# Infini-attention beside sliding-window attention: ordering the last phase by query tile

## Chip, core and metric

The kernel runs on one core of one Trainium2 chip. The metric is device time in microseconds (us) from the launch of the program to its end. A profile of one execution shows the engines: PE (TensorE), DVE (VectorE), ACT (ScalarE), POOL (GpSimd) and SP (SyncE, which here issues the DMAs).

## What is computed

Two attention layers over 2,048 tokens of width 640, 32 heads of 20, each with its own input; the results stand side by side in an output of 2048 x 1280. Cut to what matters:

```python
# A: four segments of 512; within a segment causal softmax attention, and a read of a running memory
logits = einsum('bhqd,bhkd->bhqk', qs, ks) * scale + mask
a_dot = einsum('bhqk,bhkd->bhqd', softmax(logits), vs)
a_mem = (phi(qs) @ M) / (phi(qs) @ z + 1e-06)        # phi(t) = t + 1 if t > 0 else exp(t)
o = g * a_mem + (1 - g) * a_dot                      # g = sigmoid(beta), one per head
M += phi(ks)^T vs;  z += sum(phi(ks))
out_A = o @ wo
# B: sliding window of 256 keys
scores = where(0 <= i - j < 256, q k^T * scale, -1e9)
out_B = (softmax(scores) @ v) @ wo
```

## The kernel before

The tokens are four chunks (NC = 4) of 512, each of four tiles (CT = 4) of 128. The work is eight phases, B and A in turn for chunks 0 to 3; the last phase is A, chunk 3. The 32 heads are eight groups (G) of four. A Unit (L31) is one group in one phase.

**Packs.** A Phase (L47) lists its packs. A pack is a list of entries (unit, key tile, offset, first query tile, number of query tiles) that together fill 512 columns. `scores` (from L451; matmuls at L459) computes keys x queries for four heads, each head on its own 32 rows of PE, into two PSUM buffers "Sc" of two heads each (three exist). ACT turns each into exponentials (L465) in a tile "pt" (six exist); POOL zeroes what the causal mask forbids on the diagonal block (L479). Phase A has 20 full packs. In phase A a unit's entries cover key tiles 0 to 3 with 4, 3, 2 and 1 query tiles.

**From exponentials to output.** When all packs of a unit are issued, and two packs later (LAG), `weigh` (L495) multiplies them with v: output columns are the tokens, output rows the 20 head dimensions and the softmax sum, four heads on 32 rows each (matmuls L514) into a PSUM buffer "D" (two exist, shared with all other dense work). DVE evicts it as "oc" (L527), a DMA transpose on SP's queue turns it to tokens on partitions, "ocT" (L529), and three packs later in the last phase `normalise` (L540) takes the reciprocal of the sum (L544), multiplies (L549) into "otA" and, in phase A, adds the memory's part "omem" (L561; for groups 0 to 4 together, then group by group). After group 7 the phase's four tiles are ready for output: `prefetch` turns them by DMA transposes "oT" (`turn`, L571), at most three at a time, and `out_step` computes half a tile (five matmuls L580, DVE eviction L583), with a store after the second half (L587).

**Order.** `body` (L656) issues everything by hand, pack by pack: what was put down for this slot (`after`), scores, one weighing if one is ready, prefetch, then dense work picked by cost. The dense work of the last phase is eight reads of the memory (`read`, L415: matmuls L435, DVE L442 to L445 into omem) and the output halves that OUT_TILES allows: 8 tiles here, a tile two slots after its turn at the earliest. Each engine and the SP queue work in the order of issue.

**The end.** Before the last pack's scores, groups 0 to 4 of the chunk are turned on PE (`last_turn` for column blocks 0 to 2: L616, copies L623). After them `tail` (L736) weighs groups 6 and 7, turns them on PE (`turn_here`, matmuls L536), normalises them, turns column blocks 3 and 4 (L616, L620, L621) and multiplies all four tiles with wo (`last_mm`, L628), the first three blocks in between, and stores them (L641, L643, L646).

Of the kernel before, what the change touches and what calls it, by code (L numbers as in the profile page):

```python
# [27 lines left out]
OUT_TILES = (0, 0, 3, 2, 6, 3, 7, 8)  # L28
# [3 lines left out]
class Unit:  # L32


    def __init__(self, br, c, g):
        self.br, self.c, self.g = br, c, g
        self.left = 0
        self.work = []
# [11 lines left out]
class Phase:  # L50

    def __init__(self, br, c):
# [4 lines left out]
        if br == "A":  # L57
# [20 lines left out]
        for p in self.packs:  # L78
            for e in p.entries:
                e[0].left += 1  # L80


class Kern:
# [367 lines left out]
    def scores(self, pk, last=False):  # L451
# [15 lines left out]
        for (u, kt, off, q0, nq) in pk.entries:  # L467
            loc = kt - u.c * CT
            if last:
                b = off + loc - q0  # L470
                blk = pt[:, 0:2, b * P:(b + 1) * P]
                nc.gpsimd.affine_select(out=blk, in_=blk, pattern=[[0, 2], [1, P]],
                                        compare_op=ALU.is_ge, fill=0.0, base=0,
                                        channel_multiplier=-1)
                self.open_masks.append(pt[:, 2:4, b * P:(b + 1) * P])
            elif 0 <= loc - q0 < nq:
                b = off + loc - q0
                blk = pt[:, :, b * P:(b + 1) * P]
                nc.gpsimd.affine_select(out=blk, in_=blk, pattern=[[0, 4], [1, P]],  # L479
                                        compare_op=ALU.is_ge, fill=0.0, base=0,  # L480
                                        channel_multiplier=-1)
# [6 lines left out]
        for e in pk.entries:  # L488
            u = e[0]
# [4 lines left out]

    def weigh(self, u):  # L495
        nc = self.nc
        O = self.dtile([P, CH], F32)
# [22 lines left out]
        if self.closing:  # L520
            if u.g == G - 1:
                nc.scalar.copy(out=oc[:, 0:256], in_=O[:, 0:256])
                nc.vector.tensor_copy(out=oc[:, 256:512], in_=O[:, 256:512])
            else:
                nc.vector.tensor_copy(out=oc[:], in_=O[:])
            return oc
        nc.vector.tensor_copy(out=oc[:], in_=O[:])  # L527
        tp = self.wk.tile([P, CT, P], BF16, name="ocT", bufs=4)
        nc.sync.dma_start_transpose(out=tp[:], in_=oc[:])  # L529
        late = 3 if u.br == "A" and u.c == NC - 1 else 4  # L530
        self.at(self.slot + late, lambda: self.normalise(u, tp))

    def turn_here(self, u, oc):
        tp = self.dtile([P, CT, P], BF16)
        for b in range(CT):
            self.nc.tensor.transpose(out=tp[:, b, :], in_=oc[:, b * P:(b + 1) * P],  # L536
                                     identity=self.ident[:])
        self.normalise(u, tp)

    def normalise(self, u, tp):  # L540
        nc = self.nc
        pv = tp[:].rearrange("p b (j c) -> p b j c", j=4)
        rr = self.wk.tile([P, CT, 4], F32, name="rr", bufs=2)
        nc.vector.reciprocal(out=rr[:], in_=pv[:, :, :, DH])  # L544
        if u.g == 0:
# [3 lines left out]
        nc.vector.tensor_tensor(out=o[:, :, cols].rearrange("p b (j e) -> p b j e", j=4),  # L549
                                in0=pv[:, :, :, 0:DH],  # L550
                                in1=rr[:].unsqueeze(3).to_broadcast([P, CT, 4, DH]),
                                op=ALU.mult)
        if u.br == "A" and u.c > 0:
# [6 lines left out]
            if cols.stop > cols.start:  # L560
                nc.vector.tensor_tensor(out=o[:, :, cols], in0=o[:, :, cols],  # L561
                                        in1=self.omem[:, :, cols], op=ALU.add)
        if u.g == G - 1:
            self.tiles += [(u.br, u.c, tt) for tt in range(CT)]
# [40 lines left out]
    def last_turn(self, br, c, m0, m1):  # L605

        nc = self.nc
        o = self.o_tok[br, c]
        if m0 == 0:
            self.oTs = self.wk.tile([P, KT, CT, P], BF16, name="pkt", bufs=1)  # L610
        n = 2 if m0 == 0 else 4
        for a in range(0, CT, n):
            ps = self.dtile([P, m1 - m0, n, P], BF16)
            for i in range(n):
                for m in range(m0, m1):
                    nc.tensor.transpose(out=ps[:, m - m0, i, :],  # L616
                                        in_=o[:, a + i, m * P:(m + 1) * P],
                                        identity=self.ident[:])
            if m0:
                nc.vector.tensor_copy(out=self.oTs[:, m0:m1, 0:2, :], in_=ps[:, :, 0:2, :])  # L620
                nc.scalar.copy(out=self.oTs[:, m0:m1, 2:4, :], in_=ps[:, :, 2:4, :])  # L621
            else:
                nc.vector.tensor_copy(out=self.oTs[:, m0:m1, a:a + 2, :], in_=ps[:])  # L623

    def last_mm(self, br, tt, m0, m1):
        for hf in range(2):
            for m in range(m0, m1):
                self.nc.tensor.matmul(self.last[tt][hf], lhsT=self.oTs[:, m, tt, :],  # L628
                                      rhs=self.w[br + "o"][:, m, hf * 320:(hf + 1) * 320],
                                      start=(m == 0), stop=(m == KT - 1))  # L630

    def last_sc(self, tt):
        ps = self.ps.tile([P, 2, CH], F32, name="Sc", bufs=3)
        self.last[tt] = [ps[:, 0, 0:320], ps[:, 1, 0:320]]
        return ps

    def last_store(self, br, c, tt, ps, eng):
        nc = self.nc
        ot = self.wk.tile([P, 2, 320], BF16, name="ot" if tt < 3 else "oT", bufs=3 if tt < 3 else 4)
        if eng is nc.scalar:  # L640
            nc.scalar.copy(out=ot[:], in_=ps[:, :, 0:320])  # L641
        else:
            nc.vector.tensor_copy(out=ot[:], in_=ps[:, :, 0:320])  # L643
        r0 = c * CH + tt * P
        c0 = 0 if br == "A" else D
        nc.sync.dma_start(out=self.out2d[r0:r0 + P, c0:c0 + D],  # L646
                          in_=ot[:].rearrange("p a b -> p (a b)"))
# [8 lines left out]
    def body(self):  # L656
# [3 lines left out]
        self.closing, self.open_masks = False, []  # L660
        for n, ph in enumerate(phases):
# [12 lines left out]
            for i, pk in enumerate(ph.packs):  # L674
# [7 lines left out]
                if last:  # L682
                    self.last_turn("A", NC - 1, 0, 3)
# [33 lines left out]
        self.tail("A", NC - 1)  # L717
# [18 lines left out]
    def tail(self, br, c):  # L736

        nc = self.nc
        self.closing, self.last, ps = True, {}, {}
        (_, u), (_, w) = self.ready  # L740
        assert not self.tiles
        ou = self.weigh(u)
        for blk in self.open_masks:
            nc.vector.tensor_tensor(out=blk, in0=blk,
                                    in1=self.cmask[:].unsqueeze(1).to_broadcast([P, 2, P]),
                                    op=ALU.mult)
        while self.turned or self.half:
# [5 lines left out]
        ps[0] = self.last_sc(0)  # L753
        self.last_mm(br, 0, 0, 3)
        self.turn_here(u, ou)
        ps[1] = self.last_sc(1)
        self.last_mm(br, 1, 0, 3)
        ow = self.weigh(w)
        ps[2] = self.last_sc(2)
        self.last_mm(br, 2, 0, 3)  # L760
        self.turn_here(w, ow)
        self.last_turn(br, c, 3, KT)
        for tt in range(3):
            self.last_mm(br, tt, 3, KT)
            self.last_store(br, c, tt, ps[tt], (nc.scalar, nc.vector)[tt % 2])
        ps[3] = self.last_sc(3)
        self.last_mm(br, 3, 0, KT)
        self.last_store(br, c, 3, ps[3], nc.vector)
# [50 lines left out]
```

## Time and profile before

| what | value |
|---|---|
| median of 3 runs | 392.62 us (392.05 to 395.66) |
| the profiled execution | 390.19 us |
| its span on the core | 388.1 us |
| granted PE clock | 0.99 of full speed |
| busy over the span: PE, DVE, ACT, POOL | 88%, 71%, 87%, 65% |
| first exponential of the last phase | 338.67 us |
| last two exponentials start | 373.28 and 374.20 us |
| last store issued | 385.33 us |

All times inside the profile count from the start of the span; about 2 us lie around it. A row of the order of time gives start, duration, engine, line, operation, output and inputs, and in brackets how long the engine had idled and what ended that.

### The profile page before, as it was taken

The page shows a single profiled execution, that of the slowest core. Times are in us where ns is not written, and L with a number is a line of the kernel's source. Part 1 is how long each engine was busy: PE and PEld are TensorE (multiplying, and loading weights), DVE is VectorE, ACT ScalarE, POOL GpSimd, SP SyncE. Part 2 cuts the span into 40 slices and gives each one's busy share as a digit, 9 for nine tenths or more (in the row PEclk, how much of TensorE's full clock was granted, in tenths as well). Part 3 has the DMA queues.
Part 4 walks back from the last instruction along what each step waited for, and adds up shares of the span by engine and source line. Part 5 has one row for each costly group of instructions (what it writes and reads, how often), then busy time and mean ns, then how long its engine had stood idle before and what let it go on. Part 6 is the DMA issues. An engine that isn't in the chain of part 4 may idle for free.

```text
span 388.1 us, 10554 instructions
## 1 busy us (share of the span) xinstructions
PE 340.4 (88%) x4060; PEld 161.3 (42%) x4060; DVE 276.7 (71%) x581; ACT 338.1 (87%) x384; POOL 251.8 (65%) x392
## 2 busy tenths in 40 slices
PE   7999988977998798988997989898999989988884
PEld 3433434322443344444543335444454435544442
DVE  2467667634788868788778886789877887777583
ACT  2867789985999889888999999988999999999972
POOL 9657564542777587635578888844458988955550
PEclk9999999998999989999999999999999999999999
DMA  8993328647434597728575697758474377736312
GB/s 256 314 285 77 47 83 151 113 105 187 134 80 134 143 173 141 135 71 137 117 135 135 127 190 126 149 104 110 116 146 120 92 169 129 113 78 113 96 30 70
DMA packets 110738, 50.77 MB, mean 131 GB/s; under 512 B 81760, under 2 KB 110688, under 8 KB 110688
## 3 DMA queue, kind: packets, MB, share of 16 engines
q1 hardware_dynamic: 110688, 50.10, 61.1%
q8 instruction: 32, 0.52, 0.6%
q14 instruction: 18, 0.15, 0.1%
HBM read 16.39 MB, written 14.42 MB: 79 GB/s over the span
## 4 chain that ended last, share of the span: by engine, by line
PE 42%; ACT 24%; DVE 16%; issue 6%; POOL 6%; DMA 3%; SPq 0%; POOLq 0%; DVEq 0%; ACTq 0%
ACT pt L465 22%; PE D L267 13%; PE Sc L459 7%; PE D L326 6%; PE D L580 5%; PE D L514 5%; PE D L253 4%; POOL pt L479 3%; DVE qk L270 3%; POOL pt L485 3%; DVE oc L527 3%; ACT pe L310 2%; PE Sc L628 2%; DVE omem L445 1%; DMA ocT<-oc 1%
## 5 line engine op out<-in xcount | busy, mean ns | idle before, releaser
L465 ACT ACTIVATE pt<-Sc 128x1024 bf16<-128x1024 f32 (+1 forms) x344 | 320.7, 1077 | 32.3 <-PE Sc L459 28.2
L479 POOL TENSOR_SCALAR_AFFINE_SELECT pt<-pt 128x512 bf16<-128x512 bf16 x254 | 167.6, 671 | 117.2 <-ACT pt L465 116.9
L485 POOL TENSOR_SCALAR_AFFINE_SELECT pt<-pt 128x512 bf16<-128x512 bf16 x112 | 78.6, 717 | 5.1 <-ACT pt L465 4.8
L270 DVE CAST qk<-D 128x512 bf16<-128x512 f32 x70 | 47.9, 687 | 29.4 <-PE D L267 26.8
L527 DVE CAST oc<-D 128x512 bf16<-128x512 f32 x62 | 42.7, 688 | 19.9 <-PE D L514 19.8
L459 PE MATMUL Sc<-qpB,kpB 20*128 20x256 bf16 (+2 forms) x704 | 43.3, 277 | 7.8 <-ACT pt L465 4.7
L459 PE MATMUL Sc<-qpA,kpA 20*128 20x384 bf16 (+3 forms) x512 | 41.0, 302 | 5.8 <-ACT pt L465 5.0
L580 PEld LDWEIGHTS <-oT 128*128 128x128 bf16 x280 | 25.4, 98 | 17.9 <-issue 6.6
L583 DVE CAST ot<-D 128x320 bf16<-128x320 f32 x56 | 27.0, 485 | 7.2 <-PE D L580 6.4
L459 PEld LDWEIGHTS <-kpB 20*128 20x128 bf16 x704 | 13.6, 92 | 42.5 <-issue 38.5
L267 PE MATMUL D<-xTA,Aq 128*128 128x512 bf16 x100 | 24.9, 379 | 4.6 <-DVE oc L527 3.5
L326 PE MATMUL D<-Av,xTA 128*128 128x320 bf16 x160 | 26.2, 300 | 2.8 <-DVE vA L334 1.6
L514 PE MATMUL D<-pt,vA 128*32 128x256 bf16 (+3 forms) x576 | 23.5, 287 | 5.7 <-DVE qk L270 2.2
L580 PE MATMUL D<-Bo,oT 128*128 128x320 bf16 x160 | 27.3, 306 | 1.0 <-DVE omem L445 0.4
L267 PE MATMUL D<-xTA,Ak 128*128 128x512 bf16 x100 | 25.3, 384 | 2.1 <-DVE qk L270 2.0
L326 PE MATMUL D<-Bv,xTB 128*128 128x320 bf16 x160 | 26.0, 300 | 1.4 <-DVE oc L527 0.9
L514 PE MATMUL D<-pt,vB 128*32 128x384 bf16 (+2 forms) x720 | 26.1, 277 | 0.5 <-DVE qk L270 0.3
L459 PEld LDWEIGHTS <-kpA 20*128 20x128 bf16 x512 | 11.7, 91 | 30.6 <-issue 27.9
L267 PE MATMUL D<-xTB,Bq 128*128 128x512 bf16 x75 | 19.8, 396 | 3.4 <-DVE qk L270 3.2
L549 DVE TENSOR_TENSOR otB<-ocT,rr 128x320 bf16<-128x320 bf16 x32 | 20.2, 631 | 1.1
L544 DVE RECIPROCAL rr<-ocT 128x16 f32<-128x16 bf16 x62 | 15.1, 243 | 8.0 <-DMA ocT<-oc 8.0
L580 PE MATMUL D<-Ao,oT 128*128 128x320 bf16 x120 | 20.1, 299 | 0.7 <-DVE qk L270 0.4
(84 smaller groups left out, 358.8 us busy)
## 6 DMA issues: line engine op xcount, KB each, us to landing
out_dram<-ot SPq DMA_DIRECT2D x31, 160.0 KB
kdA<-qk SPq DMA_DIRECT2D x20, 128.0 KB
qdA<-qk SPq DMA_DIRECT2D x20, 128.0 KB
kdB<-qk SPq DMA_DIRECT2D x15, 128.0 KB
qdB<-qk SPq DMA_DIRECT2D x15, 128.0 KB
kpB<-kdB SPq DMA_DIRECT2D x8, 160.0 KB
qpB<-qdB SPq DMA_DIRECT2D x8, 160.0 KB
kpA<-kdA SPq DMA_DIRECT2D x8, 160.0 KB
```

The lines of the kernel that those rows point to most:

```text
L267: nc.tensor.matmul(ps[:], lhsT=self.w[br + which][:, kt, m * P:(m + 1) * P], rhs=self.xT[br][:, kt, :], start=(kt == 0), stop=(kt == KT - 1))
L270: nc.vector.tensor_copy(out=t[:], in_=ps[:])
L326: nc.tensor.matmul(ps[:, 0:320], lhsT=self.xT[br][:, kt, tt * P:(tt + 1) * P], rhs=self.w[br + "v"][:, kt, hf * 320:(hf + 1) * 320], start ...
L459: nc.tensor.matmul(ps[j // 2][:, j % 2, off * P:(off + nq) * P], lhsT=kp[rows, u.g, k0:k0 + P], rhs=self.qp[u.br][rows, u.g, q0 * P:(q0 + ...
L465: nc.scalar.activation(out=pt[:, 2 * hp:2 * hp + 2, 0:pk.used], in_=ps[hp][:, :, 0:pk.used], func=ACT.Exp, scale=SCALE)
L479: nc.gpsimd.affine_select(out=blk, in_=blk, pattern=[[0, 4], [1, P]], compare_op=ALU.is_ge, fill=0.0, base=0, channel_multiplier=-1)
L485: nc.gpsimd.affine_select(out=blk, in_=blk, pattern=[[0, 4], [-1, P]], compare_op=ALU.is_ge, fill=0.0, base=-1, channel_multiplier=1)
L514: nc.tensor.matmul(O[32 * j:32 * j + 32, q0 * P:(q0 + nq) * P], lhsT=v[:, kt % CT, v0:v0 + 32], rhs=pt[:, j, off * P:(off + nq) * P], star ...
L527: nc.vector.tensor_copy(out=oc[:], in_=O[:])
L549: nc.vector.tensor_tensor(out=o[:, :, cols].rearrange("p b (j e) -> p b j e", j=4), in0=pv[:, :, :, 0:DH], in1=rr[:].unsqueeze(3).to_broad ...
L580: nc.tensor.matmul(ps[:, 0:320], lhsT=st["oT"][:, m, :], rhs=self.w[br + "o"][:, m, hf * 320:(hf + 1) * 320], start=(m == 0), stop=(m == K ...
L583: nc.vector.tensor_copy(out=st["ot"][:, hf * 320:(hf + 1) * 320], in_=ps[:, 0:320])
```

## The change

In the last phase the packs are put in another order. First, for each pair of groups, three packs with query tiles 0 to 2 alone; then five further sets, of groups (0,1), (2,3), (4,5), (6) and (7), with one pack per group that holds query tile 3 against all four key tiles. Such a set is an End. The number of packs stays 20.

A unit of the last phase now covers three tiles: its weighing, eviction (384 columns), transpose and normalising are of three tiles, and the one of group 7 is normalised two slots later and not three. After it tiles 0 to 2 are ready for the usual turn and output, which OUT_TILES now allows (11). `end_out` is a fourth tile row of its own in a free otB buffer. Ends of two groups are weighed with `weigh_end` (16 matmuls of 128 columns a group), turned by DMA and normalised three slots later; the one of groups 4 and 5, which is still waiting after the last scores, is turned on PE. The Ends of groups 6 and 7 are weighed by `weigh_tokens`: the exponentials are the stationary operand and 21 columns of v the moving one, so that tokens are on the partitions at once. `last_turn` turns blocks of tile 3 with plain matmuls against the identity, memory part and attention part summed in PSUM. Then come five blocks of `last_mm` for tile 3 alone, and two stores of half a tile, one from SP and one from ACT's queue.

By engine, from the recorded order of the two programs, in the last phase: output halves among the packs 17 instead of 14, and three more after the last scores; POOL the same number of masks, the last but one over four heads instead of two; DVE 16 instructions more; ACT's two copies, two evictions become one copy, one eviction and one store issue; SP: ocT transposes 8 of three blocks and 2 of two blocks where there were 6 of four, three more oT. In the last phase SP issues, from the middle on: the transpose of group 7, a store, the transpose of the first End, the turns of tiles 0 and 1, a store, the transpose of the second End, the turn of tile 2, then stores. DVE normalises groups 6 and 7 in the same slot (15), ahead of the first End's eviction.

The diff, cut (functions that are taken out are named, not shown):

```diff
-OUT_TILES = (0, 0, 3, 2, 6, 3, 7, 8)
+OUT_TILES = (0, 0, 3, 2, 6, 3, 7, 11)
...
-        if br == "A":
+        if br == "A" and c == NC - 1:
+            for a in range(0, G, 2):
+                u, w = [Unit(br, c, g, CT - 1) for g in (a, a + 1)]
+                self.packs.append(Pack([(u, t0, 0, 0, 3), (u, t0 + 2, 3, 2, 1)]))
+                self.packs.append(Pack([(u, t0 + 1, 0, 1, 2), (w, t0 + 1, 2, 1, 2)]))
+                self.packs.append(Pack([(w, t0, 0, 0, 3), (w, t0 + 2, 3, 2, 1)]))
+            for groups in ((0, 1), (2, 3), (4, 5), (6,), (7,)):
+                end = End(groups, len(groups) == 1)
+                for g in groups:
+                    u = Unit(br, c, g, 1, end)
+                    self.packs.append(Pack([(u, t0 + k, k, 3, 1) for k in range(CT)]))
+        elif br == "A":
...
+    def weigh_end(self, h):
+        nc = self.nc
+        n = len(h.groups)
+        O = self.dtile([P, CH], F32)
+        for i, ((u, kt, off, _, _), pt) in enumerate(h.work):
+            b = h.groups.index(u.g)
+            for j in range(4):
+                v0 = VW * (4 * u.g + j)
+                nc.tensor.matmul(O[32 * j:32 * j + 32, b * P:(b + 1) * P],
+                                 lhsT=self.vt["A"][0][:, kt % CT, v0:v0 + 32],
+                                 rhs=pt[:, j, off * P:(off + 1) * P],
+                                 start=(i == 0), stop=(i == len(h.work) - 1),
+                                 tile_position=(0, 32 * j))
+        oc = self.wk.tile([P, CH], BF16, name="oc", bufs=2)
+        nc.vector.tensor_copy(out=oc[:, 0:n * P], in_=O[:, 0:n * P])
+        return oc
...
+    def divide(self, pv, dst, n):
+        nc = self.nc
+        rr = self.wk.tile([P, CT, 4], F32, name="rr", bufs=2)
+        r = rr[:].rearrange("p b j -> p (b j)")[:, 0:n]
+        nc.vector.reciprocal(out=r, in_=pv[:, :, DH])
+        nc.vector.tensor_tensor(out=dst.rearrange("p (h e) -> p h e", e=DH), in0=pv[:, :, 0:DH],
+                                in1=r.unsqueeze(2).to_broadcast([P, n, DH]), op=ALU.mult)
+
+    def weigh_tokens(self, h):
+        nc = self.nc
+        O = self.dtile([P, 4, VW], F32)
+        g = h.groups[0]
+        for heads, keys in (((0, 1), 3), ((0, 1), 4), ((2, 3), 3), ((2, 3), 4)):
+            for (_, kt, off, _, _), pt in h.work[keys - 1:keys] if keys == 4 else h.work[:3]:
+                for j in heads:
+                    v0 = VW * (4 * g + j)
+                    nc.tensor.matmul(O[:, j, 0:DH + 1], lhsT=pt[:, j, off * P:(off + 1) * P],
+                                     rhs=self.vt["A"][0][:, kt % CT, v0:v0 + DH + 1],
+                                     start=(j == 0 and off == 0), stop=(j == 3 and off == 3))
+        self.divide(O, self.end_out()[:, GW * g:GW * (g + 1)], 4)
...
     def weigh(self, u):
         nc = self.nc
+        if isinstance(u, End):
+            oc = self.weigh_end(u)
+            tp = self.wk.tile([P, CT, P], BF16, name="ocT", bufs=4)
+            nc.sync.dma_start_transpose(out=tp[:, 0:2, :], in_=oc[:, 0:2 * P])
+            self.at(self.slot + 3, lambda: self.end_normalise(u, tp))
+            return
...
-        nc.vector.tensor_copy(out=oc[:], in_=O[:])
+        n = u.tiles
+        nc.vector.tensor_copy(out=oc[:, 0:n * P], in_=O[:, 0:n * P])
...
-        late = 3 if u.br == "A" and u.c == NC - 1 else 4
+        late = (2 if u.g == G - 1 else 3) if u.br == "A" and u.c == NC - 1 else 4
...
+    def last_turn(self, m0, m1):
+        nc = self.nc
+        n = m1 - m0
+        ps = self.dtile([P, n, P], F32)
+        for i in range(n):
+            cols = slice((m0 + i) * P, (m0 + i + 1) * P)
+            for k, src in enumerate((self.omem[:, CT - 1, cols], self.end_out()[:, cols])):
+                nc.tensor.matmul(ps[:, i, :], lhsT=src, rhs=self.ident[:],
+                                 start=(i == 0 and k == 0), stop=(i == n - 1 and k == 1))
+        return ps
...
+    def tail(self):
+        nc = self.nc
+        (_, e45), (_, e6), (_, e7) = self.ready
+        oc = self.weigh_end(e45)
+        while self.tiles or self.turned or self.half:
+            self.prefetch()
+            self.out_step()
...
+        tp = self.dtile([P, 2, P], BF16)
+        for b in range(2):
+            nc.tensor.transpose(out=tp[:, b, :], in_=oc[:, b * P:(b + 1) * P],
+                                identity=self.ident[:])
+        self.end_normalise(e45, tp)
+        self.weigh_tokens(e6)
+        t0 = self.last_turn(0, 3)
+        oT = self.wk.tile([P, KT, CT, P], BF16, name="pkt", bufs=1)
+        nc.vector.tensor_copy(out=oT[:, 0, 0:3, :], in_=t0[:])
+        for blk in self.open_masks:
+            nc.vector.tensor_tensor(out=blk, in0=blk,
+                                    in1=self.cmask[:].unsqueeze(1).to_broadcast([P, 2, P]),
+                                    op=ALU.mult)
+        self.last = self.ps.tile([P, 2, CH], F32, name="Sc", bufs=3)
+        for m in range(3):
+            self.last_mm(m, oT[:, 0, m, :])
+        t3 = self.last_turn(3, 4)
+        oT3 = self.wk.tile([P, CH], BF16, name="phik", bufs=3)
+        nc.scalar.copy(out=oT3[:, 0:P], in_=t3[:, 0, :])
+        self.weigh_tokens(e7)
+        self.last_mm(3, oT3[:, 0:P])
+        t4 = self.last_turn(4, 5)
+        oT4 = self.wk.tile([P, CH], BF16, name="phik", bufs=3)
+        nc.vector.tensor_copy(out=oT4[:, 0:P], in_=t4[:, 0, :])
+        self.last_mm(4, oT4[:, 0:P])
+        for hf in range(2):
+            ot = self.wk.tile([P, D], BF16, name="ot", bufs=3)
+            src = self.last[:, hf, 0:320]
+            dst = self.out2d[S - P:S, 320 * hf:320 * (hf + 1)]
+            if hf == 0:
+                nc.vector.tensor_copy(out=ot[:, 0:320], in_=src)
+                nc.sync.dma_start(out=dst, in_=ot[:, 0:320])
+            else:
+                nc.scalar.copy(out=ot[:, 0:320], in_=src)
+                nc.scalar.dma_start(out=dst, in_=ot[:, 0:320])
```

`end_normalise` is `divide` over two groups (8 heads). Taken out: `turn_here`, the old `last_turn`, `last_mm`, `last_sc`, `last_store` and the old `tail`.

## The prediction

> **What bounds the kernel now.** I read the page, then the last phase by windows, then the chain that ended last and the order of time in its last 15 us, and last the SP queue. The windows are the last phase's 20 packs of exponentials, in two halves, and what follows the last of them.
>
> ```profile
> core 0: us, PE busy (x) PEld busy (x) DVE busy (x) ACT busy (x) POOL busy (x), PEclk, DMA share, GB/s
> 338.67:356.80 18.13, 15.70 (x209) 7.77 (x206) 14.03 (x38) 18.13 (x22) 10.92 (x18) 1.00 0.46 94
> 356.80:375.53 18.73, 15.12 (x193) 7.61 (x192) 13.59 (x30) 18.73 (x21) 11.77 (x18) 1.00 0.31 75
> 375.53:388.14 12.61, 7.21 (x74) 4.61 (x71) 5.32 (x13) 2.34 (x5) 0.00 (x0) 1.00 0.16 54
> ```
>
> ACT is busy without a gap through the phase; PE has 16% to spare, DVE 25%. Then come 12.6 us without exponentials. The chain says what they are:
>
> ```profile
> 374.34 0.73 PE D L514 x16
> 375.06 0.92 PE Sc L628 x6
> ...
> 378.66 0.32 PE D L536 x4
> ...
> 379.29 0.50 DVE otA L549
> ...
> 379.82 0.33 DVE otA L561
> ...
> 381.28 3.18 PE Sc L628 x22
> ...
> 384.48 0.82 DVE oT L643
> ```
>
> The end is PE's: the last weighings, transposes and 40 output matmuls. The change takes part of this into the phase, where the price depends on DVE and on DMA transposes. Their rows (the two SP rows and the first DVE row from about 75 us, the others from the end):
>
> ```profile
> 71.72 3.84 SPq L571 DMA_TRANSPOSE oT<-otB  x3
> 77.34 1.20 SPq L529 DMA_TRANSPOSE ocT<-oc  x1
> ```
> ```profile
> 79.77 0.25 DVE L544 RECIPROCAL rr<-ocT 128x16 f32<-128x16 bf16 x1 [2.74 <-DMA ocT<-oc]
> ```
> ```profile
> 369.21 0.49 DVE L583 CAST ot<-D 128x320 bf16<-128x320 f32 x1
> 370.42 1.30 DVE L561 TENSOR_TENSOR otA<-otA,omem 128x1600 bf16<-128x1600 bf16 x1
> 372.32 0.83 DVE L549 TENSOR_TENSOR otA<-ocT,rr 128x320 bf16<-128x320 bf16 x1
> 375.12 0.69 DVE L525 CAST oc<-D 128x512 bf16<-128x512 f32 x1 [0.37 <-PE D L514]
> 376.59 0.49 DVE L549 TENSOR_TENSOR otA<-D,rr 128x320 bf16<-128x320 bf16 x1
> ```
>
> A transpose holds the SP queue 1.2 us, three in a row 3.84, and its data are usable 2.43 us after its start (77.34 to 79.77). DVE's multiply takes 0.49, or 0.83 to 0.96 beside POOL's masks.
>
> **The pack's rhythm.** Exponentials of pack 0 start at 338.67, of pack 19 at 373.28: 1.82 us a pack. With three Sc buffers the scores of a pack finish only after the first exponential of the pack before (1.33 us), so PE has about 1.5 us a pack for anything else before ACT waits.
>
> **PE in the phase.** A half output tile costs 0.79 (368.32 to 369.10), two 1.46 (351.17 to 352.63). Before has 14 halves in the phase, after 17; three stay after the last scores. Six weighings of 0.66 become eight of 768 columns instead of 1,280 (0.46) and two of the new weigh_end (0.5); the early turn of 0.9 goes. So 2.4 - 0.9 + 0.7 = +2.2 us on 30.8: it still fits 36.8 in sum. Score matmuls of 128 columns, 16 a pack, stream the same columns; the 8-matmul packs take 0.33 to 0.5, and I take 0.45. POOL keeps its number of masks.
>
> **DVE in the phase.** Added: three more evictions of 0.49, eight 384-column evictions (between the rows of 256 at 0.43 and 512 at 0.69: 0.56) and two of 0.43 for six of 0.69, two more normalisations, two more adds of omem, one new normalisation; the two copies of 0.54 go. About +3.4 on 27.6 us: 84%, but unevenly. Packs 12 to 15 hold: normalise of group 4 with the add of 1,200 elements (0.28 + 0.4 + 1.0, overlapped 1.5; 1.25 to 1.75), eviction, read (0.98); then group 5, eviction, half tile; two half tiles; then groups 6 and 7 together (0.87 each, up to 1.3 beside POOL) and an eviction. D has two buffers and DVE works in order, so PE waits behind these.
>
> Count from the first exponential of pack 12; packs 0 to 11 I find on time, DVE being at most 0.1 late. DVE ends group 4 at 1.5, evicts group 6 by 2.1, ends the read at 3.0. PE can weigh group 7 at 2.1 and start a half tile, which needs the read's D, only at 3.0; scores of pack 14 start at 3.8 and its exponentials at 4.3, due 3.64: **0.7 lost**. Pack 15 likewise 6.36 for 6.16: **0.2 lost**. Group 7's transpose, issued at 4.4 and usable at 6.8, is there when DVE comes to it at 7.2, so normalising one pack earlier costs nothing. Then DVE does groups 6 and 7 from 6.4 to 8.1 and evicts the first End at 8.5. SP, in order, issues its transpose 8.6 to 9.8 and only then the turn of tile 0, 9.8 to 11.1, landing 2.57 after its start (as at 71.72) at 12.4; tile 1's lands at 13.7. Pack 17's PE list is scores, weigh_end, then two halves of tile 0, which it would start at 10.4. It waits 2.0, and 0.5 is over the 1.5 us anyway: exponentials of pack 18 start at 14.4 instead of 11.8, **2.6 lost**. Behind those halves stand the scores of pack 18, and ACT waits for them. On SP tile 2's turn stands behind a store and the second End's transpose: issued 14.0, landed 16.6, used in the end at 17.4, hidden by the same wait. Pack 19 starts at 16.25, against 12.74 without waits: 3.5 us late.
>
> Bounds of this: the End's transpose moves two blocks; four and five both cost 1.2, the shortest SP issue is 0.34. I take 1.2, nearest in kind. A landing can take 4.3 (the third at 71.72). Contended DVE adds 0.9. So 3.5, from 1.6 to 6.
>
> **The end.** From the first exponential of pack 19, before needs 388.14 - 373.28 = 14.85. After: weigh_end to 0.44; three halves to 2.66, paced by D; DVE evicts the last by 3.25 and normalises two Ends (0.55 each) to 4.3; PE meanwhile weighs group 6 by tokens, 16 pairs, 3.3 to 4.15; six transposing matmuls (0.06 each and 0.2 latency) to 4.9; copy 0.56 to 5.5 (the mask multiply of 0.28 behind it is done long before group 7 is weighed); six output matmuls of 0.136 to 6.4; two transposes, group 7's 16 pairs to 7.4; reciprocal and multiply 0.5 to 8.0; two transposes 8.3; copy 0.3 to 8.7; two matmuls 9.2; eviction 0.49 to 9.7; the store from 9.73. From the last store's issue (385.33) to the end before takes 2.80, so 12.5. That saves 2.3. Unknown: the pairs with 21 columns. Five reads, of which two have 21 columns, take 0.37 with latency, loads 0.05 apiece (35 in 1.7 us). I take 0.05 a pair; 0.026, the gap after a 21-column matmul, to 0.074 (transposes, 0.89 for 12) gives -0.4 to +0.4 each weighing. ACT's own store queue is in no row; SP's issue of 0.33 to 0.77 bounds it, 0 to +0.4. Saving 1.3 to 3.2.
>
> [...]
>
> **Sum.** +3.5 - 2.3 = +1.2 us. The profiled execution (390.19, of which 388.1 span) would become 391.4; the median of the runs shown stands 2.4 above it, so the prediction is 392.62 + 1.2 = 393.8.
>
> **Rivals.** *The turned tile comes in time.* If pack 17's halves find their transpose landed, 2.0 of the 2.6 goes and perhaps the 0.9 of packs 14 and 15: -0.8 to -2.3, so 390.3 to 391.8. It decides if the turn is issued by 7.8, two microseconds earlier. For it: DVE's idle share; against: two normalisations and an eviction stand ahead of the End's transpose, and that ahead of the turn.
>
> *DVE becomes the bound (the slower side).* If multiplies go at 0.9 instead of 0.49 because POOL is beside them, six normalisations from pack 9 on cost 0.41 more each and the adds of omem 0.3 each: 2.5 + 1.2 = 3.7, uncovered as DVE is over 90% booked there; 393.8 + 3.7 = 397.5. It decides when the mean multiply passes 0.8; the mean of before's six otA rows in the phase is 0.63, which speaks half against it.
>
> *More gain than counted:* no wait in the phase and an end shorter by 1.6 more gives 388.7. Every price in the end would have to be at its lower bound.
>
> **How the numbers follow.** Forecast 0.62, the tile in time 0.17, DVE the bound 0.15, more gain 0.06. About 1% (3.9 us) is what a measurement of this kernel can tell from no change. Faster: 0.06. Slower: the DVE case, and a little of the forecast's upper end (6 lost, 1.3 saved: +4.7), 0.17 in all. Same: 0.77. The range takes the bounds of the forecast and most of the first rival: 390.3 to 397.0; the forecast's own range is 391.6 to 396.5.
>
> **What would show it.** ACT idle of some 2.5 us before pack 18, ended by PE scores, with PE waiting for the DMA of oT; smaller gaps before 14 and 15, ended by DVE; first exponential of pack 19 to the end of the span near 12.5. Wrong if the oT row on SP starts within 1.5 us of pack 15's first exponential, if weighing by tokens takes over 1.5 us, or if ACT has no gap.

## The result and the profile after

| | before | after |
|---|---|---|
| median | 392.67 us (20 runs) | 397.16 us (20 runs, 394.26 to 399.82) |
| ratio, 95% interval | | 1.0105, 1.0074 to 1.0135 |
| the profiled execution | 390.19 | 397.57 |
| its granted PE clock | 0.991 | 0.963 |
| first exponential of pack 0 | 338.67 | 340.12 |
| from there to that of pack 19 | 34.61 | 43.14 |
| from there to the end of the span | 14.85 | 12.34 |

The kernel is 4.1 us (by the ratio) to 4.5 us (by the medians) slower, where +1.2 was forecast. The median of 397.16 lies just above the range's upper end of 397.0; by the ratio, from the 392.62 that the prediction started from, it would be 396.7, just below that end. By the prediction's own measure of what can be told from no change (about 1%, 3.9 us), the result stands on the border. Ratios here, and the line through all runs further down, leave out the few executions more than 1.5% above the fastest of their kernel; medians hold all.

Of the difference between the two profiled executions, 1.45 us lie before the last phase, where the two programs are the same. The change's own account is +8.5 in the packs and -2.5 in the end. The execution of before that was profiled (390.19) is among that kernel's fastest, so 8.5 is measured against a favourable pass.

The windows of the kernel after, cut like those of before: packs 0 to 9, the other ten packs, and what follows the last exponential.

```profile
core 0: us, PE busy (x) PEld busy (x) DVE busy (x) ACT busy (x) POOL busy (x), PEclk, DMA share, GB/s
340.12:358.36 18.24, 16.53 (x250) 8.48 (x250) 14.70 (x43) 18.24 (x21) 13.12 (x22) 1.00 0.42 100
358.36:385.50 27.14, 21.82 (x343) 11.97 (x336) 14.16 (x40) 19.26 (x21) 8.62 (x14) 0.75 0.33 77
385.50:395.60 10.10, 4.49 (x59) 2.89 (x57) 4.12 (x14) 0.69 (x2) 0.00 (x0) 0.92 0.16 50
```

The first ten packs are untouched: ACT has no gap. The next ten take 27.1 us for 19.3 us of exponentials. The column to look at is PEclk: 0.75, where before had 1.00 in all three rows. The chain of waits in that stretch now runs mostly through PE, and once through a DMA:

```profile
354.71 1.79 ACT pt L486 x2
360.34 2.79 PE D L646 x10
368.58 2.18 PE D L646 x10
371.21 1.51 ACT pt L486 x2
374.67 3.07 DMA oT<-otA
377.78 2.85 PE D L646 x10
383.98 2.22 PE D L646 x15
```

Ten matmuls on L646 are two output halves. They cost 1.46 before; here two pairs take 2.8 and 2.85. The lines around pack 18, in order of time, for PE, SP and ACT:

```profile
374.45 0.63 PE L525 MATMUL D<-pt,vA 128*32 128x128 bf16 x32
377.78 2.85 PE L646 MATMUL D<-Ao,oT 128*128 128x320 bf16 x10 [2.71 <-DMA oT<-otA]
380.56 0.61 PE L480 MATMUL Sc<-qpA,kpA 20*128 20x128 bf16 x16
```
```profile
373.45 1.17 SPq L567 DMA_TRANSPOSE ocT<-oc  x1
374.67 3.02 SPq L637 DMA_TRANSPOSE oT<-otA  x2
```
```profile
381.27 3.01 ACT L486 ACTIVATE pt<-Sc 128x1024 bf16<-128x1024 f32 x3 [4.46 <-PE Sc L480]
```

Read them in this order: SP issues the first End's transpose at 373.45 and only then, at 374.67, the turn. PE has finished its weighing by 375.1 and waits 2.71 for the DMA. It then computes two halves at half speed and after them the scores of pack 18. ACT waits 4.46 for these.

The granted clock, stretch by stretch:

```profile
core 0: us, PE busy (x) PEld busy (x) DVE busy (x) ACT busy (x) POOL busy (x), PEclk, DMA share, GB/s
353.00:356.50 3.50, 3.08 (x51) 1.63 (x42) 2.54 (x7) 3.50 (x5) 2.44 (x4) 1.00 0.41 102
356.50:359.70 3.20, 2.33 (x48) 1.17 (x45) 3.05 (x11) 3.20 (x5) 2.03 (x4) 1.00 0.58 133
359.80:363.10 3.30, 3.30 (x20) 1.42 (x23) 1.16 (x3) 2.63 (x3) 2.18 (x4) 0.50 0.52 103
363.20:366.60 3.40, 2.16 (x66) 1.26 (x59) 3.23 (x10) 2.98 (x4) 1.22 (x2) 1.00 0.16 53
366.70:369.90 3.20, 3.20 (x27) 1.60 (x26) 1.52 (x4) 1.89 (x3) 0.63 (x1) 0.50 0.31 62
370.00:376.80 6.80, 4.12 (x123) 2.48 (x120) 3.89 (x11) 6.22 (x7) 1.91 (x3) 1.00 0.19 48
...
373.40:376.80 3.40, 1.19 (x49) 0.77 (x48) 0.93 (x3) 3.40 (x4) 1.15 (x2) 1.00 0.24 48
...
376.90:383.60 6.70, 5.82 (x67) 3.12 (x71) 1.91 (x5) 2.28 (x3) 0.89 (x2) 0.50 0.50 117
```

In this trace the clock is 1.00 or 0.50 and nothing between, and in this phase each stretch at 0.50 lasts 3.4 us or twice that (3.41 and 6.83). The first two follow stretches in which PE was busy 2.33 of 3.20 and 2.16 of 3.40 us, with weighings, reads and scores and hardly any output half. The third is different: in the 3.4 us ahead of it PE was busy 1.19 us only, as it stood waiting for the turned tile from 375.07 on. In the three rows at half clock PE is busy for 3.30, 3.20 and 5.82 us and ACT for 2.63, 1.89 and 2.28: there PE is the busy engine and ACT the waiting one.

### The profile page after: what moved, and what is told of

It is laid out like the page before. It is cut to its first block, busy times and chain, and to the rows that moved or that the text cites. A ratio compares the mean times of both kernels' runs of the same rounds, so it can differ in the third digit from the quotient of the medians.

```text
span 395.6 us, 10936 instructions
## 1 busy us (share of the span) xinstructions
PE 348.2 (88%) x4236; PEld 165.2 (42%) x4236; DVE 275.1 (70%) x597; ACT 337.2 (85%) x382; POOL 250.6 (63%) x392
## 4 chain that ended last, share of the span: by engine, by line
PE 40%; ACT 26%; DVE 16%; issue 6%; POOL 5%; DMA 4%; SPq 1%; POOLq 0%; ACTq 0%; DVEq 0%
ACT pt L486 24%; PE D L288 12%; PE D L646 7%; PE Sc L480 6%; PE D L347 4%; PE D L587 4%; PE D L274 4%; POOL pt L500 3%; DVE qk L291 3%; DVE oc L594 3%; ACT pe L331 2%; POOL pt L506 2%; DMA ocT<-oc 1%; DVE omem L466 1%; PE D L231 1%
## 5 line engine op out<-in xcount | busy, mean ns | idle before, releaser
L594 DVE CAST oc<-D 128x512 bf16<-128x512 f32 (+1 forms) x64 | 42.9, 670 | 18.8 <-PE D L587 18.7
L480 PE MATMUL Sc<-qpA,kpA 20*128 20x128 bf16 (+3 forms) x608 | 40.4, 289 | 5.6 <-ACT pt L486 5.3
L649 DVE CAST ot<-D 128x320 bf16<-128x320 f32 x62 | 30.1, 487 | 16.1 <-PE D L646 15.3
L646 PEld LDWEIGHTS <-oT 128*128 128x128 bf16 x310 | 29.6, 103 | 24.5 <-issue 7.6
L646 PE MATMUL D<-Bo,oT 128*128 128x320 bf16 x160 | 29.7, 327 | 1.0 <-DVE rr L610 0.5
L646 PE MATMUL D<-Ao,oT 128*128 128x320 bf16 x150 | 26.9, 317 | 3.1 <-DMA oT<-otA 2.7
L288 PE MATMUL D<-xTA,Ak 128*128 128x512 bf16 x100 | 27.1, 405 | 2.1 <-DVE qk L291 2.0
L587 PE MATMUL D<-pt,vA 128*32 128x256 bf16 (+3 forms) x544 | 22.0, 283 | 4.3 <-DVE qk L291 2.2
L288 PE MATMUL D<-xTB,Bk 128*128 128x512 bf16 x75 | 19.8, 397 | 0.8 <-DVE omem L466 0.6
L610 DVE RECIPROCAL rr<-ocT 128x16 f32<-128x16 bf16 (+1 forms) x64 | 15.3, 240 | 6.6 <-DMA ocT<-oc 6.6
```

The costliest lines, as they stand in the source:

```text
L288: nc.tensor.matmul(ps[:], lhsT=self.w[br + which][:, kt, m * P:(m + 1) * P], rhs=self.xT[br][:, kt, :], start=(kt == 0), stop=(kt == KT - 1))
L480: nc.tensor.matmul(ps[j // 2][:, j % 2, off * P:(off + nq) * P], lhsT=kp[rows, u.g, k0:k0 + P], rhs=self.qp[u.br][rows, u.g, q0 * P:(q0 + ...
L587: nc.tensor.matmul(O[32 * j:32 * j + 32, q0 * P:(q0 + nq) * P], lhsT=v[:, kt % CT, v0:v0 + 32], rhs=pt[:, j, off * P:(off + nq) * P], star ...
L594: nc.vector.tensor_copy(out=oc[:, 0:n * P], in_=O[:, 0:n * P])
L646: nc.tensor.matmul(ps[:, 0:320], lhsT=st["oT"][:, m, :], rhs=self.w[br + "o"][:, m, hf * 320:(hf + 1) * 320], start=(m == 0), stop=(m == K ...
L649: nc.vector.tensor_copy(out=st["ot"][:, hf * 320:(hf + 1) * 320], in_=ps[:, 0:320])
```

## The experiments

The theory after the result: the prediction's waits are there, somewhat above the predicted size, and the rest is the half clock, which the new order brings on because it leaves stretches without output halves. The main rival: the waits themselves (SP, DVE, D buffers) are longer than predicted, and the clock is a by-product. The table gives, for every run, what the first exponentials of neighbouring packs stand apart beyond 1.82 us ("late", from 0.1 us up), in the one profiled execution. It shows the packs of one execution each; the ratio stands on all runs. Line numbers in the experiments are those of their own kernels.

| kernel | packs 0 to 19 | end | late before packs 11 to 16 | 17 to 19 | ratio to before, 95% |
|---|---|---|---|---|---|
| before | 34.61 | 14.85 | 0 | 0 | |
| after | 43.14 | 12.34 | 3.76 | 4.78 | 1.0105 (1.0074 to 1.0135) |
| after, once more | 41.91 | 12.72 | 2.12 | 5.14 | 1.0126 (1.009 to 1.0162) |
| no late tiles | 37.82 | 15.61 | 3.30 | 0 | 1.0082 (1.0047 to 1.0117) |
| fill | 41.33 | 12.41 | 2.06 | 4.69 | 1.0086 (1.0042 to 1.013) |
| turns first | 42.46 | 11.83 | 4.24 | 3.69 | 1.0077 (1.0039 to 1.0114) |
| one half a pack | 39.19 | 13.56 | 0.16 | 4.47 | 1.0052 (1.0013 to 1.0091) |
| paced end | 36.17 | 14.67 | 1.70 | 0 | 1.001 (0.9977 to 1.0043) |
| paced end with fill | 35.67 | 12.91 | 1.19 | 0 | 0.9959 (0.9924 to 0.9993) |
| no late tiles with fill | 37.48 | 15.63 | 2.81 | 0 | 1.0123 (1.0076 to 1.0169) |
| before with fill | 36.30 | 14.41 | 0 (1.38 before packs 7, 8) | 0.49 | 0.9977 (0.9945 to 1.001) |
| more fill | 39.71 | 12.84 | 2.06 | 3.04 | 1.0031 (0.9995 to 1.0066) |

**No late tiles.** The tiles of the last phase's own chunk are not multiplied among the packs; all six halves go to the end.

```diff
-                can = 2 * sum(1 for t in self.turned if t[0] + 2 <= self.slot) + len(self.half)
+                can = 2 * sum(1 for t in self.turned if t[0] + (9 if t[1][:2] == ("A", NC - 1) else 2)
+                              <= self.slot) + len(self.half)
```

> The three halves of tiles 0 and 1 of the last chunk are kept out of the packs and stand after the last scores. Theory (pack 18 waits 4.6 us, of which 2.6 for the turned tile's DMA, 1.4 because two halves then run at half clock): the gap before pack 18 goes to under 0.5, three more halves in the end cost about 2.1, or 4 if at half clock; some 2 us faster than the changed kernel, 1.006 or so against the kernel before. Rival (the time is lost to DVE, the DMA wait is only where it shows): a gap of 2 us or more stays before pack 18 or moves to pack 19, and the time does not fall.

The wait ahead of pack 18 is gone, 4.61 to 0, and the end pays 3.3 us for it. So that wait belongs to the halves of the turned tile. The time hardly falls: 1.0082 against 1.0105 and 1.0126 of the kernel after, with overlapping intervals. The clock:

```profile
361.70:365.00 3.30, 2.22 (x60) 1.25 (x62) 3.01 (x8) 3.30 (x5) 2.62 (x5) 1.00 0.50 122
365.10:371.80 6.70, 6.35 (x91) 3.32 (x82) 3.87 (x12) 3.92 (x5) 1.67 (x3) 0.50 0.23 56
```

It falls to half here too, 5 us later than in the kernel after, and packs 14 and 15 are now 3.3 late together. This slow stretch does not come from the turned tile.

**Fill.** Two useless full-array matmuls of 512 columns ahead of the weighing of groups 4, 5 and 6, overwritten by it. In the trace each pair is a row of PE of 0.59 to 0.61 us.

```diff
+        if u.tiles < CT and u.g in (4, 5, 6):
+            for _ in range(2):
+                nc.tensor.matmul(O[:], lhsT=self.w["Bo"][:, 0, 0:P], rhs=self.w["Ao"][:, 0, 0:CH],
+                                 start=True, stop=True)
```

> Two matmuls of 512 columns on the whole array are put ahead of the weighings of groups 4, 5 and 6 (packs 9, 10, 12), overwritten by the weighing: 1.3 us of useless work for PE. Theory (PE's clock is halved for 3.4 us after a stretch with little matmul work, and the halves of packs 11 to 14 then take twice as long): the half clock near packs 11 and 14 goes, the gaps before packs 12, 14 and 15 fall from 3.5 to under 1.5 us in sum, 2 us faster than the changed kernel in spite of the added work; the wait at pack 18 stays. Rival (DVE's order makes these gaps, the clock has no part): the same or up to 1.3 us slower.

```profile
340.15:375.10 34.95, 28.83 (x500) 15.30 (x496) 27.45 (x74) 33.49 (x37) 20.15 (x33) 1.00 0.38 89
375.20:381.90 6.70, 5.90 (x71) 3.21 (x75) 1.91 (x5) 2.36 (x3) 0.99 (x2) 0.50 0.48 113
```

With more work on PE, the clock stays full until 375 and packs 11 to 16 are late by 2.06 instead of 3.76. The 1.0 us that remains ahead of pack 12 at full clock is not the clock's. PE waits there for D behind DVE, whose multiply takes 0.80 and 0.89 (the last experiment, where it is nearly the same, shows the lines). How much of this 1.0 us the useless matmuls themselves cause, two pairs of which stand just ahead, was not separated. The packs take 1.8 and 0.6 us less than in the two profiles of after, but the time, expected to fall by 2 us, cannot be told from that kernel's (1.0086).

**Turns first.** SP gets the turns ahead of the End's transpose.

```diff
+                if n == len(phases) - 1:
+                    self.prefetch()
                 if self.ready and self.ready[0][0] <= self.slot:
```

> In the last phase the turns of finished tiles are issued ahead of the weighing of the same pack, so that on the DMA queue they no longer stand behind the first End's transpose. Theory (the queue's order costs one transpose of 1.2 us, plus its wait for the eviction, 0.5): the wait for the turned tile at pack 17 falls by 1.5 to 1.7 us from 2.7, and the time by 1.5 to 3 with the half clock that the wait brings. Rival (the turn waits for the normalising of group 7 anyway): under 0.5.

```profile
373.57 3.05 SPq L637 DMA_TRANSPOSE oT<-otA  x2
376.71 1.20 SPq L567 DMA_TRANSPOSE ocT<-oc  x1
```
```profile
377.28 2.85 PE L646 MATMUL D<-Ao,oT 128*128 128x320 bf16 x10 [1.79 <-DMA oT<-otA]
```

PE's wait falls from 2.71 to 1.79, 0.9 us where 1.5 to 1.7 was expected; from issue to use it is 3.7 here against 3.1. The order on SP is part of the wait, not all of it, and the pair that follows still takes 2.85. The time was to fall by 1.5 to 3 us; by the ratios it fell by about 1 (1.0077), which is not clear of noise.

**One half a pack.** The planner may take one output half in a pack of the last phase and not three, which spreads the halves.

```diff
-                                      mem[at[1]:at[1] + 3], min(outs - at[2], can, 3),
+                                      mem[at[1]:at[1] + 3],
+                                      min(outs - at[2], can, 1 if n == len(phases) - 1 else 3),
```

> At most one output half in a pack of the last phase, so that they lie in every pack and not in pairs; a half moves into the end (4 there, not 3). Theory (pairs overrun the 1.5 us a pack, and packs without halves let the clock fall): no gap over 0.5 before packs 12 to 15, no half clock until the wait at pack 17, which stays but is followed by one half only; 3 to 4 us faster than the changed kernel. Rival (DVE is the bound): the gaps spread over packs 9 to 16 and stay 3 us in sum.

Packs 11 to 16 are late by 0.16 us in all, without any useless work; the clock is 1.00 until 371.5. With the same halves one at a time, the clock stayed up in these packs and PE did not stand behind D there. By the ratio the kernel stands about 2 us below the kernel after (1.0052, the intervals just overlap), where 3 to 4 was expected. What is late next shows in two lines of PE:

```profile
370.76 0.84 PE L646 MATMUL D<-Bo,oT 128*128 128x320 bf16 x5 [1.75 <-DVE oc L531]
...
375.16 1.52 PE L646 MATMUL D<-Ao,oT 128*128 128x320 bf16 x5 [2.04 <-DMA oT<-otA]
```

Now that the packs come on time, group 7, normalised one slot earlier by the change, makes DVE wait for its transpose (0.41 us, at 368.95), and the End's eviction and PE wait behind it. The wait on the turned tile stays.

**Paced end.** One half a pack, no late tiles, group 7 normalised after three slots as the others, and the six halves of the end spread between its other steps, in free Sc buffers, evicted by ACT.

```diff
-        late = (2 if u.g == G - 1 else 3) if u.br == "A" and u.c == NC - 1 else 4
+        late = 3 if u.br == "A" and u.c == NC - 1 else 4
...
-        while self.tiles or self.turned or self.half:
-            self.prefetch()
-            self.out_step()
+        half(0, 0)
+        half(0, 1)
...
         self.end_normalise(e45, tp)
+        half(1, 0)
+        half(1, 1)
         self.weigh_tokens(e6)
```

> One half a pack, no half of tiles 0 to 2 of the last chunk among the packs, group 7 normalised three packs later; these six halves go into the end, through the Sc buffers and ACT, between the steps that wait for DVE. Theory: first to last pack 34.6 to 36, as nothing waits for a turned tile and pairs are gone; the end from pack 19 12.5 to 13.5; in sum 48 against 49.5 before and 55.5 in the changed kernel, so 1 us faster than the kernel before, unless the clock falls after pack 14 and the end runs at half speed (then 2 to 3 us more). Rival (DVE is the bound): gaps of over 2 us stay in packs 9 to 17.

The loss is gone: 1.001 (0.9977 to 1.0043). The kernel was to be 1 us faster than before unless the clock fell. No wait on a turned tile is left, but the end is 14.67, partly at half clock:

```profile
358.60:378.30 19.70, 15.96 (x320) 9.14 (x321) 13.07 (x35) 18.52 (x21) 8.68 (x14) 0.82 0.41 91
378.30:391.10 12.80, 8.68 (x82) 5.62 (x79) 3.35 (x12) 3.00 (x6) 0.00 (x0) 0.87 0.23 67
```

**Paced end with fill.** The same with useless pairs of 512 columns in packs 14, 16, 17 and 18.

```diff
+                if n == len(phases) - 1 and i in (14, 16, 18, 18):
+                    self.fill(self.dtile([P, CH], F32))
...
+        if h.groups[0] == 2:
+            self.fill(O)
```

> The same with two useless matmuls of 512 columns on the whole array in packs 14, 16, 17 and 18, 0.43 us each, where no output halves are left. Theory: no half clock from pack 14 to the end, up to 2 us faster than without them, 1.5 to 2 us faster than the kernel before. Rival (clock has no price): no difference, or slower by up to 1 us.

```profile
359.60:378.76 19.16, 16.09 (x337) 9.36 (x336) 13.21 (x35) 18.51 (x21) 8.94 (x14) 1.00 0.40 94
378.76:389.80 11.04, 6.13 (x74) 4.17 (x71) 3.26 (x12) 2.89 (x6) 0.00 (x0) 0.91 0.32 76
```

Eight useless matmuls, and the end is 12.91 instead of 14.67; the median is 390.41, against 392.97 without them and 392.57 for the kernel before. With and without them the mean times stand 2.1 us apart, with a standard error of 0.7, in runs taken side by side: more work on PE made the kernel faster. It is the fastest of all versions, 0.9959 (0.9924 to 0.9993), within 1% of the kernel before.

**No late tiles with fill**, the first two edits together.

> The changed kernel with both single edits: halves of tiles 0 and 1 after the last scores, and the useless matmuls in packs 9, 10 and 12. Theory (the two losses add): gaps of 1.0, 0.9 and 0.1 before packs 12, 14, 15, as with the useless matmuls alone, and none at 18: first to last pack 36.7, against 43.1 in the changed kernel; end 14 to 16. Rival (they share a cause): no better than the better one alone, 37.8.

```profile
355.70:359.10 3.40, 2.48 (x44) 1.24 (x43) 3.30 (x9) 3.40 (x5) 2.34 (x5) 1.00 0.54 125
359.20:362.50 3.30, 3.30 (x27) 1.69 (x27) 1.78 (x5) 1.44 (x2) 2.18 (x4) 0.50 0.40 80
```

This one speaks against a simple reading: the useless matmuls are in, and the clock falls at 359 all the same. The packs take 37.48, where the theory said 36.7 and either edit alone gave 41.33 and 37.82; the time (1.0123, six runs) is no better than with either edit alone. The slow stretches lie differently in the traces: one begins at 359.8 in after, at 365.1 with no late tiles, at 375.2 with fill and at 359.2 here. The runs of one program differ as well: the mean clocks of the 20 of after go from 0.959 to 0.980.

**After, once more**, to see how far one profile of the same kernel differs from the next.

> The changed kernel once more, unaltered, beside the others on one chip: 396 to 398, gaps before packs 12, 14, 15 and 18, the last the largest by far, and half clock in windows of 3.4 us whose place may differ.

Pack 12 is late by 1.47 and pack 18 by 5.14, as in the first profile (1.43 and 4.61); packs 14 and 15 by 0.65 and not 2.14. The mean clock of the execution is 0.974 here and 0.963 there, so what one program meets of the half clock varies by execution.

**Before with fill.** Is the lead of the paced version the new order's?

```diff
+                if n == len(phases) - 1 and i in (14, 16, 17, 18):
+                    self.fill(self.dtile([P, CH], F32))
```

> The kernel before, with two useless full-array matmuls of 512 columns into a spare D buffer at the ends of packs 14, 16, 17 and 18; the output is unchanged. It asks whether the gain of the paced version with useless work belongs to the new order or would come in the old one too. Theory (the old order already carries an output half in nearly every one of these packs, so its last phase keeps the full clock): nothing to win, the matmuls cost 0 to 0.43 us a pack where PE has no slack, so the median is 0 to 1.5 us above the kernel before, and the last phase's first-to-last exponential stays at 34.6 to 36. Rival (useless work helps any order): the median falls by 1.5 us or more, and the paced version's lead over the kernel before is not the new order's.

```profile
347.70:351.10 3.40, 2.61 (x27) 1.20 (x26) 3.20 (x9) 3.40 (x5) 2.02 (x3) 1.00 0.21 43
351.20:354.50 3.30, 3.03 (x33) 1.57 (x34) 1.87 (x5) 2.90 (x4) 2.02 (x3) 0.50 0.41 99
```

0.9977 (0.9945 to 1.001): no gain that can be told from none; first to last pack is 36.30, just above the expected 34.6 to 36. The rows are from before the first useless matmul: the old order meets the half clock too, in this execution at packs 7 and 8. The interval overlaps with that of the paced version with fill, so the runs do not settle how much of that version's lead is the order's.

**More fill.** The fill experiment, with two pairs more ahead of the second End's weighing and one at the end of pack 16, so that PE works while the tile is turned.

```diff
+        if h.groups[0] == 2:
+            self.fill(O)
+            self.fill(O)
...
+                if n == len(phases) - 1 and i == 16:
+                    self.fill(self.dtile([P, CH], F32))
```

> The changed kernel with the useless matmuls of the fill experiment (groups 4, 5, 6), and four more ahead of the second End's weighing and two at the end of pack 16, so that PE is not idle while it waits for the turned tile; the output is unchanged. Theory (the half clock explains what the prediction's steps leave over): no stretch at half clock from pack 0 to the first exponential of pack 18; pack 18 late by 2.6 to 3.4 (the transposes stay, the pair of halves takes 1.5 and not 2.85), packs 12 to 15 together by 0.9 to 2; first exponential of pack 0 to that of pack 19 38.2 to 40, median 393 to 394.5. Rival (the waits are DVE's and SP's, the clock is only a by-product): pack 18 stays 4.5 late or more, and the median stays at 395 or above.

```profile
340.64:358.80 18.16, 16.80 (x243) 8.56 (x241) 14.61 (x41) 18.16 (x22) 13.24 (x22) 1.00 0.41 97
358.80:382.10 23.30, 18.24 (x351) 10.56 (x353) 15.77 (x43) 18.92 (x21) 8.59 (x15) 1.00 0.39 92
382.10:393.20 11.10, 5.56 (x59) 3.42 (x57) 4.12 (x14) 0.89 (x3) 0.00 (x0) 0.81 0.15 47
```
```profile
361.30 1.75 PE L658 MATMUL D<-Bo,oT 128*128 128x320 bf16 x10 [0.75 <-DVE oc L606]
...
376.57 1.53 PE L658 MATMUL D<-Ao,oT 128*128 128x320 bf16 x10 [1.48 <-DMA oT<-otA]
```
```profile
357.49 0.87 DVE L627 TENSOR_TENSOR otA<-ocT,rr 128x240 bf16<-128x240 bf16 x1
...
359.89 0.89 DVE L627 TENSOR_TENSOR otA<-ocT,rr 128x240 bf16<-128x240 bf16 x1
```

In the profile this run separates the two theories. The packs run at full clock throughout; pack 18 is late by 3.04 (2.6 to 3.4 expected; the rival said 4.5), with the pair of halves at 1.53. Packs 12 to 15 keep 2.06, just above the expected 0.9 to 2. So the packs cost 5.1 us more than before at full clock (39.71 - 34.61), the useless matmuls' own time included, and by difference about 3.4 of the 8.5 in the profile of after are put down to the half clock: 0.6 at packs 11 and 12, 1.1 at 14 and 15, 1.7 at 18 and 19. This compares single executions. The median, 395.12, did not come down to the 393 to 394.5 expected and stands where the rival put it (395 or above); but before stood at 393.79 beside it, so it is +1.3 us. Its ratio, 1.0031 (0.9995 to 1.0066), lies below both intervals of the kernel after (from 1.0074 and 1.009 up): twelve useless matmuls more, and about 3 us less.

**All runs by their clock.** Every run has a mean granted clock. One line with a common slope through 72 runs of before beside the experiments and the 26 of after (both labels) has 257 us per unit of clock. Before has a mean clock of 0.983, after 0.970, so 3.2 of the 4.2 us between the means go with the clock, and 1.0 us (standard error 0.3) remains at equal clock. By the same line the paced end stands at -1.6, with fill at -2.6, before with fill at +0.1. This is a correlation and no proof, but it agrees with the fills.

## Where the prediction held and where it failed, point by point

The direction held, and so did the shorter end and the mechanism of the wait ahead of pack 18. The size did not: +4.1 to +4.5 where +1.2 was forecast. That the time still comes out at the edge of the range is partly luck, as that range was built from longer waits, and the half clock, which came on top, is in none of its bounds.

- **"PE in the phase ... it still fits": the step that failed.** All matmuls were priced at the speed of the trace of before, where the last phase ran at clock 1.00. The sum of PE's work was about right; its rate was not. A pair of halves at half clock takes 2.85, not 1.46, and this stands on the path each time. By the difference above it cost 3.4 us in the profile of after, and it stands in no term of the sum and in no rival.
- **"Packs 0 to 11 I find on time": wrong by the pack behind them.** Packs 0 to 10 are on time. Pack 12 is late by 1.43 in after, where PE was at half clock and DVE's multiplies took 0.41. With fill, at full clock, it is late by 1.01, where they took 0.80 to 0.89 and a pair of halves waits for D, with the useless matmuls ahead of it. Spreading the halves, without useless matmuls, takes both away (one half a pack: 0).
- **Packs 14 and 15, 0.7 and 0.2.** Measured 1.44 and 0.70 at half clock, 0.92 and 0.13 at full clock, beside useless matmuls. The count of DVE's work was near.
- **Pack 18, 2.6.** The mechanism was right: the turn is issued 3.46 after pack 15's first exponential (9.8 - 6.36 = 3.44 predicted), behind the End's transpose. It landed after 3.07 and not 2.57, and the two turns held SP for 3.02. At full clock the pack is 3.04 late; in after 4.61, with the half clock.
- **The end, 12.5.** Measured 12.34. Sixteen pairs of the weighing by tokens took 0.55 us, not 0.85:

```profile
386.76 0.55 PE L557 MATMUL D<-vA,pt 128*128 128x21 bf16 x16 [0.47 <-DVE ot L649]
387.71 0.23 PE L679 MATMUL D<-ident,omem 128*128 128x128 bf16 x1 [0.40 <-DVE otB L545]
```

  That is 0.034 us for a load of 128 columns and its matmul (0.55 over 16), the last one's latency included, where the prediction took 0.05.
- **The rivals.** The turned tile did not come in time. DVE became a bound at one place only, pack 12 at full clock, for 1.0 us and not 3.7. The slower side happened, by a mechanism that none of them named. The first rival's lower figure does not follow from its own terms: without the 2.0 and the 0.9 the sum is -1.7, so 390.9; -2.3 (390.3) needs every wait gone.
- **The sum.** Predicted 3.5 - 2.3 = +1.2. In the profiles: 5.1 at full clock, 3.4 for the half clock, -2.5 for the end, +6.0; the medians differ by 4.5. The first and the last of these lie within the bounds given for them (1.6 to 6 and 1.3 to 3.2); those bounds together reach +4.7, 397.3, and not the 396.5 that was given as the forecast's upper end. The single profiles exceed the medians, and part of that is probably that the one profiled execution of before had a clean last phase, which not all of its runs have: with fill, the old order was late by 1.4 at packs 7 and 8, ahead of the first useless matmul. The prediction should have asked what held the clock at 1.00 there; the last section has what was measured of it.

## What to carry to other kernels

Before pricing matmuls from a trace, look at the granted clock of the stage, and at what the clock does once the work is moved. Here the change bunched the large matmuls, and the rate of those that remained was halved in places although the busy sums fitted: the clock of packs 10 to 19 was 0.75 and not 1.00, and a pair of halves took up to 2.85 us and not 1.46. What holds the clock up was not shown; the last section has the stretches that were counted. Spread dense work one piece a pack rather than in pairs (packs 11 to 16 were late by 0.16 us and not 3.76), and test the clock by adding useless large matmuls: when more work makes the kernel shorter, as by 2.1 us between the two paced versions, the clock is the likely cause. Where a moved DMA feeds an engine that works in order, count what stands ahead of it on its own queue; at full clock that part of the sum held to within half a microsecond (2.6 against 3.04).

## What the runs showed of the hardware that was not expected

In the packs of after the clock was at 0.50 from 359.77 to 363.18, from 366.60 to 370.01 and from 376.84 to 383.66: twice 3.41 us, and once 6.83. These places differ from one execution to the next: the profiled pass of before has 1.00 in all of its packs, while that of before with fill, whose first useless matmul comes only at pack 14, has 0.50 from 351.2 on.

PE need not be idle in the stretch ahead of it. It was busy 74% and 64% of the 3.41 us ahead of the first two in after, and its longest wait ahead of the first was 0.48 us. Its busy share alone does not decide, though. These two stretches of the last kernel, one after the other, had some 94% and 60%, and the clock stayed at 1.00 in and behind both:

```profile
361.60:365.00 3.40, 3.19 (x59) 1.61 (x58) 2.84 (x7) 2.73 (x4) 1.98 (x4) 1.00 0.52 125
365.00:368.40 3.40, 2.05 (x42) 1.31 (x41) 3.25 (x10) 2.61 (x4) 1.27 (x2) 1.00 0.16 34
```

Stretches of before and after can also be told apart by how many output matmuls they hold (the matmuls of 128 x 320, five to a half). A matmul that reaches over the edge of a stretch is counted in both:

| stretch at full clock | PE busy | output matmuls | clock of the next |
|---|---|---|---|
| after, 352.94 to 356.36 | 88% | 10 | 1.00 |
| after, 356.36 to 359.77 | 74% | 0 | 0.50 |
| after, 363.18 to 366.60 | 64% | 1 | 0.50 |
| after, 370.01 to 373.42 | 86% | 11 | 1.00 |
| after, 373.42 to 376.84 | 34% | 1 | 0.50 |
| before, 359.03 to 362.44 | 79% | 8 | 1.00 |
| before, 369.27 to 372.68 | 79% | 5 | 1.00 |
| before, 372.68 to 376.10 | 68% | 6 | 1.00 |

The other stretches at full clock in the packs of these two traces hold 5 to 11 and were followed by 1.00. This is a sorting found afterwards, in one phase of one execution of each kernel, and no run varied this count alone. What sets the clock was not shown. Nor does this tell how near the old order is to losing it: its profiled pass held 1.00 behind a stretch busy 68%, and the pass of before with fill lost it behind one busy 77% (2.61 of 3.40).
